# Relative-bias attention and a mixture of adapters on one core: uncast loads in 1 KB runs with Pool casting, 1024-column exp groups, and the probability-value product in a two-bank tile

## The chip, the cores and the metric

The kernel runs on one core of one Trainium2 chip. The metric is the device time of one execution in microseconds (us); smaller is better. Where several runs are given, the number is their median. The engines are called PE (TensorE, matrix products), ACT (ScalarE), Vector (DVE in the profile), Pool (GpSimd), and Sync (SP); each works through its own instructions in order. A DMA is issued by one of these engines and then carried out by the DMA engines.

A run is called slow when it is more than 1.5% above the fastest run of the same kernel. Ratios below are the mean time of one kernel's fast runs over that of the other's fast runs of the same rounds on the same chip, so they are not quite the ratios of the medians that are quoted. The interval behind a ratio is a 95% one.

## The reference

```python
# q, k, v: (B=8, H=8, S=576, D=64) float32; bias_table: (32, 8)
scores = (1 / sqrt(D)) * q @ k.T
scores = scores + bias_table[bucket(|i - j|)]          # one bucket from a distance of about 128 on
attn   = softmax(scores) @ v
x      = attn.transpose(0, 2, 1, 3).reshape(4608, 512)
logits = x @ w_gate                                    # 8 experts, the best 2 are kept
w      = softmax of the 2 kept logits
out    = x + sum over the 2 experts of w * ((x @ A[e]) @ B[e])   # A: 512x16, B: 16x512
```

The output is 4608 x 512 float32.

## The kernel before

The kernel walks over 32 pairs of heads, 4 pairs in each of 8 batches. For a pair, PE makes the scores, ACT takes the exponential out of PSUM into bf16 tiles `p`, Vector multiplies the part near the diagonal by a table of exponentials of the bias (the "band"), PE multiplies by `v` with a column of ones appended, and Vector divides by the sum that this column gives (the "normalisation"). The adapter part of the previous batch is cut into pieces, and the loop puts one piece behind a score group while pieces are left. The last 64 tokens of each head (576 = 4 x 128 + 64) are the "tail" and are handled two heads at a time.

Loads go through Pool and are cast from float32 to bf16 by the DMA:

```python
def load(dst, src, b, h0, h1, cols=None):
    for j in range(4):                     # 128 tokens on 128 partitions, 4 such blocks
        o = dst[:, j, h0:h1, :D]
        nc.gpsimd.dma_start(
            out=o, in_=src[b, h0:h1, j * 128:(j + 1) * 128, :]
            .rearrange("h p d -> p h d"))
```

The band multiply has both inputs in SBUF (the on-chip memory). The normalisation comes in two parts, because PV fills two PSUM tiles:

```python
nc.vector.tensor_tensor(pm[:, :, q0:q1], pm[:, :, q0:q1],
                        Mh[:, :, x0:x0 + q1 - q0], op=ALU.mult)          # the band
...
nc.vector.reciprocal(rc, acc[:, :, :, D])                                # norm_main: 3 blocks
nc.vector.tensor_tensor(x[:, 0:3, 2 * hp:2 * hp + 2, :], acc[:, :, :, :D],
                        rc.unsqueeze(3).to_broadcast((128, 3, 2, D)), op=ALU.mult)
...                                                                      # norm_rest: 2 blocks, with a mask
```

The output of an adapter tile goes through one of three SBUF buffers and is stored by Sync's queue, which carries nothing else after the start:

```python
op = ctx.enter_context(tc.tile_pool(name="outs", bufs=3))
...
o = op.tile([128, Dm], FP32, name="o", tag="o")
nc.vector.tensor_tensor(o, ps, xs[b][:, t].rearrange("p h d -> p (h d)"), op=ALU.add)
nc.sync.dma_start(out=out[n0:n0 + 128, :], in_=o)
```

In an odd batch a fifth tile follows, with the tails of two batches (`m_outt`, output `o<-dlt`); it takes a buffer from the same three.

The main loop, cut:

```python
for i in range(NPAIR + 1):
    b, hp = divmod(i, HP)                                # HP = 4
    if hp == 0 and b + 1 < B:                            # next batch's loads
        alloc_nat(b + 1); load_tails(b + 1); load_kq(b + 1, 0, H)
    ...
    for g in range(5):
        sc = qk(i, g); softmax_exp(i, g, sc)             # 4 groups of 1152 columns, 1 of 640
        if g == 0: transposes(i + 1)
        if g == 1: norm_main(i - 1, pv_main(i - 1))
        if g == 2: norm_rest(i - 1, pv_rest(i - 1))      # hp == 0: queue += pieces(previous batch)
        if g in (0, 3, 4) and queue: queue.pop(0)()
        band(i, g)
```

The softmax here doesn't subtract the row's maximum and nothing guards it: scores larger than these inputs give would overflow.

## Time and profile before

The time before is a median of 259.1 us (258.2 to 260.7, three runs).

| | before |
|---|---|
| profiled span | 257.7 us |
| first exp / second exp start | 28.6 / 30.2 us |
| normalisation of the first pair / of the last pair starts | 37.9 / 240.1 us |
| one pair on average, from pair 4 to pair 31 | 6.60 us |
| drain after the last normalisation | 17.6 us |

The page's first part gives, for each engine, the busy microseconds, their share of the span and the number of instructions:

```profile
PE 189.7 (74%) x2576; PEld 120.1 (47%) x2576; DVE 205.9 (80%) x641; ACT 165.4 (64%) x174; POOL 117.3 (46%) x155
```

Its second part cuts the span into 40 equal slices and gives the busy share of each in tenths (9 is 90% or more):

```profile
PE   0020698797878868897799778987898788888852
...
DVE  3200678999898888999979898989998889989972
ACT  2000469897769767886688677867796678868100
POOL 8997999745733591185508560549052000000000
```

In the first four slices only Pool is busy throughout, issuing loads and preparing tiles; from the seventh on Vector stands at 7 to 9, mostly 8 or 9, until the drain. The page also names the chain of work that ended last, as shares of the span by engine:

```profile
DVE 50%; PE 26%; ACT 7%; POOL 6%; issue 5%; DMA 3%; ACTq 0%; POOLq 0%; DVEq 0%
```

Half of the chain is Vector and almost none is DMA. Two windows of two batches each show the same. The columns are the window, its length, busy microseconds (and instructions) of PE, PEld, Vector, ACT and Pool, the granted PE clock, the DMA engines' busy share, and GB/s:

```profile
54.50:109.00 54.50, 45.60 (x660) 29.46 (x659) 49.10 (x153) 41.78 (x45) 26.49 (x33) 1.00 1.12 100
109.00:163.50 54.50, 46.15 (x638) 29.43 (x638) 48.75 (x152) 40.44 (x44) 26.08 (x32) 0.97 1.15 107
```

Vector is busy about 49 of 54.5 us, PE 46. Two lines of the waits (who waited for whom: us in total, times, longest): Vector's main wait was for PE's PV product:

```profile
DVE rcA L347 <- PE pvA L304: 9.9, 25, 1.4
...
DVE o L457 <- DMA out_dram<-o: 0.8, 1, 0.8
```

Last, from the timeline (start, duration, engine, line, operation), the first exp, a band multiply alone, and one next to a cast on Pool:

```profile
28.63 1.13 ACT L275 ACTIVATE p_227<-sc 128x1152 bf16<-128x1152 f32 x1 [23.40 <-PE sc L262]
...
31.48 0.42 DVE L289 TENSOR_TENSOR p_227<-p_227,M 128x512 bf16<-128x512 bf16 x1
...
36.40 0.60 POOL L214 CAST Bb<-B_f 128x512 bf16<-128x512 f32 x1
...
36.49 0.80 DVE L289 TENSOR_TENSOR p_282<-p_282,M 128x512 bf16<-128x512 bf16 x1
```

The same multiply took 0.42 us alone and 0.80 us when it began 0.09 us after a Pool cast had.

### The profile page before, as it was taken

What the parts mean: (1) busy time and instruction counts of PE and PEld (TensorE: products, weight loads), DVE (VectorE), ACT (ScalarE), POOL (GpSimd) and SP (SyncE); (2) the same over time, 40 slices, a digit from 0 to 9 for tenths busy, and PEclk for the clock granted to TensorE, in tenths of its full rate; (3) what the DMA queues carried; (4) which work ended last, traced back from release to release, by engine and by line L of the source; (5) the groups of instructions that cost most, each with busy time, mean ns of one, the idle gap of its engine ahead of it and who ended that gap; (6) DMA issues with size and microseconds to landing.
All of it is one profiled execution on the core that took longest, in us unless ns stands there. A gap on an engine that the chain in (4) does not pass through costs nothing.

```text
span 257.7 us, 6522 instructions
## 1 busy us (share of the span) xinstructions
PE 189.7 (74%) x2576; PEld 120.1 (47%) x2576; DVE 205.9 (80%) x641; ACT 165.4 (64%) x174; POOL 117.3 (46%) x155
## 2 busy tenths in 40 slices
PE   0020698797878868897799778987898788888852
PEld 0010255465545655456356554564465544664710
DVE  3200678999898888999979898989998889989972
ACT  2000469897769767886688677867796678868100
POOL 8997999745733591185508560549052000000000
PEclk9999999999999999999889999999999999999965
DMA  4999999969893999399939992799969003202205
GB/s 27 141 154 153 94 131 114 137 42 99 85 201 54 105 84 84 122 146 85 163 95 107 58 142 34 133 166 101 147 109 69 0 3 123 84 3 83 85 21 183
DMA packets 124759, 25.56 MB, mean 99 GB/s; under 512 B 118960, under 2 KB 119992, under 8 KB 124728
## 3 DMA queue, kind: packets, MB, share of 16 engines
q0 software_dynamic: 112768, 14.16, 89.6%
q1 hardware_dynamic: 11960, 10.97, 14.6%
q8 instruction: 20, 0.33, 0.5%
q14 instruction: 11, 0.09, 0.1%
HBM read 29.84 MB, written 9.45 MB: 152 GB/s over the span
## 4 chain that ended last, share of the span: by engine, by line
DVE 50%; PE 26%; ACT 7%; POOL 6%; issue 5%; DMA 3%; ACTq 0%; POOLq 0%; DVEq 0%
PE pvA L310 11%; DVE x L348 6%; PE sc L262 5%; DVE x L360 3%; DVE kqT L250 3%; DMA vn_86<-in_v_dram 3%; DVE o L457 3%; DVE xT L377 3%; PE pvA L304 2%; PE kqps L247 2%; DVE rcA L347 2%; POOL qn L69 2%; DVE rmB L358 2%; PE sc L258 1%; PE dl L455 1%
## 5 line engine op out<-in xcount | busy, mean ns | idle before, releaser
L262 PE MATMUL sc<-kqT 64*128 64x512 bf16 x256 | 51.8, 402 | 0.0
L69 POOL DMA_DIRECT2D kn<-in_k_dram x36 | 31.2, 896 | 19.1 <-PE kqps L247 18.2
L69 POOL DMA_DIRECT2D qn<-in_q_dram x36 | 31.0, 906 | 1.6 <-DMA vn_86<-in_v_dram 1.5
L258 PE MATMUL sc<-tlT_184,kqT 128*128 128x128 bf16 x64 | 14.5, 226 | 18.3 <-DVE kqT L250 13.0
L69 POOL DMA_DIRECT2D vn_87<-in_v_dram x16 | 14.0, 894 | 28.4 <-PE pvB L336 28.4
L69 POOL DMA_DIRECT2D vn_86<-in_v_dram x16 | 14.0, 896 | 27.7 <-PE pvB L336 27.6
L262 PEld LDWEIGHTS <-kqT 64*128 64x128 bf16 x256 | 12.4, 93 | 26.5 <-issue 17.4
L250 DVE COPY kqT<-kqps 128x1024 bf16<-128x1024 bf16 x32 | 21.8, 683 | 3.5 <-PE kqps L247 3.4
L457 DVE TENSOR_TENSOR o<-dl,x 128x512 f32<-128x512 f32 x32 | 21.8, 683 | 1.6 <-DMA out_dram<-o 0.8
L258 PEld LDWEIGHTS <-kqT 128*128 128x128 bf16 x128 | 12.8, 100 | 17.7 <-DVE kqT L250 13.2
L348 DVE TENSOR_TENSOR x<-pvA,rcA 128x384 bf16<-128x384 f32 x32 | 17.8, 557 | 1.1
L455 PE MATMUL dl<-Bb,zT 128*128 128x512 bf16 x32 | 13.3, 421 | 6.8 <-DVE zT L449 2.8
L275 ACT ACTIVATE p_227<-sc 128x1152 bf16<-128x1152 f32 x1 | 1.1, 1131 | 23.4 <-PE sc L262 23.4
L239 DVE COPY tlT_184<-tps 64x512 bf16<-64x512 bf16 x8 | 3.4, 419 | 15.4 <-POOL tlT_184 L221 15.3
L258 PE MATMUL sc<-tlT_186,kqT 128*128 128x128 bf16 x64 | 14.2, 222 | 1.7 <-ACT p_571 L275 0.7
L360 DVE TENSOR_TENSOR x<-pvB,rmB 128x256 bf16<-128x256 f32 x32 | 13.6, 424 | 1.1
L347 DVE RECIPROCAL rcA<-pvA 128x6 f32<-128x6 f32 x32 | 6.2, 195 | 10.1 <-PE pvA L304 9.9
L247 PE MATMUL kqps<-ident,kn 128*128 128x128 bf16 x128 | 13.3, 229 | 1.0 <-DVE o L457 0.6
L412 ACT ACTIVATE ex<-df 128x32 f32<-128x32 f32 (+1 forms) x12 | 2.7, 222 | 17.0 <-DVE df L409 17.0
L234 PE MATMUL tps<-ident,tl 128*128 128x128 bf16 x32 | 3.4, 232 | 13.3 <-DMA tl<-in_q_dram 13.3
L247 PE MATMUL kqps<-ident,qn 128*128 128x128 bf16 x128 | 13.1, 228 | 0.0
L247 PEld LDWEIGHTS <-kn 128*128 128x128 bf16 x128 | 8.2, 101 | 7.5 <-issue 6.8
(1431 smaller groups left out, 655.4 us busy)
## 6 DMA issues: line engine op xcount, KB each, us to landing
out_dram<-o SPq DMA_DIRECT2D x32, 256.0 KB, 2.1
kn<-in_k_dram POOLq DMA_DIRECT2D x28, 128.0 KB, 4.1
qn<-in_q_dram POOLq DMA_DIRECT2D x28, 128.0 KB, 4.7
vn_86<-in_v_dram POOLq DMA_DIRECT2D x16, 128.0 KB, 5.1
vn_87<-in_v_dram POOLq DMA_DIRECT2D x16, 128.0 KB, 4.4
out_dram<-o SPq DMA_DIRECT2D x8, 128.0 KB, 4.6
Mr<-g_d SPq DMA_DIRECT2D x1, 576.0 KB, 6.6
tl<-in_k_dram POOLq DMA_DIRECT2D x8, 64.0 KB, 4.0
```

The costliest lines, as they stand in the source:

```text
L69: nc.gpsimd.dma_start(out=o, in_=src[b, h0:h1, j * 128:(j + 1) * 128, :] .rearrange("h p d -> p h d"))
L247: nc.tensor.transpose(ps[:, w, j * 128:(j + 1) * 128], n[:, j, 2 * hp:2 * hp + 2, :], ident)
L250: nc.vector.tensor_copy(t, ps)
L258: nc.tensor.matmul(sc[:, 1024:1152], lhsT=t[:, 0, g * 128:(g + 1) * 128], rhs=tt[:, hp, 1, :], start=True, stop=True)
L262: nc.tensor.matmul(sc[:, h * 512:(h + 1) * 512], lhsT=t[s, 0, g * 128:(g + 1) * 128], rhs=t[s, 1, :], start=True, stop=True)
L310: nc.tensor.matmul(acc[:, qb, h, :], lhsT=p[:, o:o + 128], rhs=vn[:, g, 2 * hp + h, :], start=first, stop=False, skip_group_check=True)
L347: nc.vector.reciprocal(rc, acc[:, :, :, D])
L348: nc.vector.tensor_tensor(x[:, 0:3, 2 * hp:2 * hp + 2, :], acc[:, :, :, :D], rc.unsqueeze(3).to_broadcast((128, 3, 2, D)), op=ALU.mult)
L360: nc.vector.tensor_tensor(x[:, 3:5, 2 * hp:2 * hp + 2, :], acc[:, :, :, :D], rm.unsqueeze(3).to_broadcast((128, 2, 2, D)), op=ALU.mult)
L377: nc.vector.tensor_copy(xT[:, :, half * 256:(half + 1) * 256], ps)
L455: nc.tensor.matmul(ps, lhsT=zT[:, t, :], rhs=Bb, start=True, stop=True)
L457: nc.vector.tensor_tensor(o, ps, xs[b][:, t].rearrange("p h d -> p (h d)"), op=ALU.add)
```

## The change

The change has two halves.

**The load half.** Four consecutive tokens lie on one partition, so a head's q or k row block comes in runs of 1 KB. The loads are uncast float32, issued by Sync, and Pool casts one pair ahead of use. The order of tokens inside a block of 128 is therefore permuted; the bias tables are built in that order, and each output tile is stored by four DMAs. `v` is loaded uncast as well, by 16 DMAs of 32 partitions. The weights of the adapters are loaded at pair 1, behind the loads for batch 1, and cast on Pool at pair 2. Pool also builds the bias tables of pairs 1 to 3, one pair ahead, which Vector built before.

**The compute half.** Every pair has five exp groups of 1024 columns; tail against tail is done once per batch. PV has a PSUM tile of its own over two banks and one normalisation of 640 columns. Band multiplies are issued one group late. Three operations of the gate go from Vector to Pool.

The core of the diff (cut; PV's inner loops, table building and start order are left out):

```diff
-            nc.gpsimd.dma_start(
-                out=o, in_=src[b, h0:h1, j * 128:(j + 1) * 128, :]
-                .rearrange("h p d -> p h d"))
+    def load_kq(b, h0, h1):
+        for t, src in zip(kfs[b], (k, q)):
+            nc.sync.dma_start(
+                out=t[:, h0:h1, :],
+                in_=src[b, h0:h1, :S4, :].rearrange("h (p j) d -> p h (j d)", j=4))
+    def load_v(b, h0, h1):
+        vr = v[b, h0:h1, :S4, :].rearrange("h (t p j) d -> j t p h d", t=4, j=4)
+        for j in range(4):
+            for t in range(4):
+                nc.sync.dma_start(out=vfs[b][j * 32:(j + 1) * 32, t, h0:h1, :], in_=vr[j, t])
+    knp = ctx.enter_context(tc.tile_pool(name="nat", bufs=3))
+    def cast_kq(i, engs=None):
+        t = knp.tile([128, 2, 4, 2, D], BF16, name="kqn", tag="kqn")
+        for w in range(2):
+            o = t[:, w].rearrange("p j h d -> p h j d")
+            s = kfs[b][w][:, 2 * hp:2 * hp + 2, :].rearrange("p h (j d) -> p h j d", j=4)
+            nc.gpsimd.tensor_copy(o, s)                  # first pair: Vector and ACT instead
+    def cast_v(i):
+        nc.gpsimd.tensor_copy(vns[b % 2][:, :, h, :D], vfs[b][:, :, h, :])
 ...
-        n = 1152 if g < 4 else 640
+        p = pp.tile([128, 2 * S4], BF16, name=f"p{g}", tag=f"p{g}")
+        nc.scalar.activation(p, sc, ACT.Exp, scale=scale)
 ...
+    def norm(i):
+        nc.vector.reciprocal(rc, at(acc, D, (SLOT, 5), (D1, 2)))
+        nc.vector.tensor_tensor(rm, rc, mask, op=ALU.mult)
+        nc.vector.tensor_tensor(xs[b][:, :, 2 * hp:2 * hp + 2, :],
+                                at(acc, 0, (SLOT, 5), (D1, 2), (1, D)),
+                                rm.unsqueeze(3).to_broadcast((128, 5, 2, D)), op=ALU.mult)
 ...
-        nc.vector.tensor_tensor(df, lg, ...)             # and two more operations of the gate
+        nc.gpsimd.tensor_tensor(df, lg, ...)
 ...
-        nc.sync.dma_start(out=out[n0:n0 + 128, :], in_=o)
+        orr = out[n0:n0 + 128, :].rearrange("(u j) d -> j u d", j=4)
+        for j in range(4):
+            nc.sync.dma_start(out=orr[j], in_=o[j * 32:(j + 1) * 32])
 ...
+            if i == 1:
+                load_weights()
             if hp == 0 and b + 1 < B:
+                load_kq(b + 1, 0, H)
+                load_v(b + 1, 0, H)
+                load_tails(b + 1)
+            if i + 2 < NPAIR:
+                cast_kq(i + 2)
+            cast_v(i)
+            if i == 2:
+                cast_weights()
```

## The prediction

> **What bounds it now.** From the busy tenths and timeline:
> (1) Start: the first exp begins at 28.6 us. The chain of waits runs through Pool: casting loads (0.9 us per issue), then the tail tiles, cleared only at 24.4.
> (2) Steady state: in three two-batch windows from 54.5 to 218 (6.8 us per pair) Vector is busy 49.1, 48.8 and 49.9 of 54.5 us, PE 46, ACT 41. Its one sizeable listed wait is the PV reciprocal on PE (8.9 us in 164). Vector is the limit.
> (3) Drain: from 238.7, 19 us of serial MoE pieces.
>
> **On Vector, per pair** (group means; instructions overlap, so one removed is worth its mean less 70 ns):
> - normalisation 195+557+176+162+424 becomes one reciprocal, one mask, one 640-column multiply (estimate from the slope 424 to 557: 825): -0.14 us;
> - group 3's extra band multiply (215): -0.15;
> - tail copies 419+419+424 per batch become one of 683: -0.11; a new 512-column tail band: +0.09;
> - three gate operations move: -0.13.
> Together -0.44 of 6.1. Later bands and PV's own banks should remove most of the reciprocal wait: -0.2.
>
> **Taken back.** Pool gains three casts per pair; casts of this size took 662 and 603 ns. The Trainium skill (SBUF — State Buffer, "Who interferes with whom") says that a Vector instruction with two SBUF inputs contends with a Pool instruction that reads SBUF; the later one blocks. The trace agrees once: the band multiply at 36.5, during a Pool cast, took 796 ns against 420. With 1.9 us of casts and five bands per pair I estimate +0.2 to 0.5. Net about -0.45 us per pair, 28 pairs: -13 us.
>
> **ACT and PE.** Exps go from 4x1131+~705 to 5x~1025 ns plus a quarter of a 512-column exp: neutral. PE keeps its matmul count.
>
> **Start.** q and k need no Pool for loading. Packets in the trace: 2 KB 86 ns, 768 B 41; my estimate is 48 for 1 KB, 18 for 256 B uncast, so batch 0 needs about 11 us on 16 engines. But pair 1's transposes stand before the second score group on PE and need heads 2 to 7, queued behind all of v: second exp at about 18, not 30. About -10 us.
>
> **New waits.** Loads and stores now share one queue. The Trainium skill (DMA: Bandwidth & Descriptors, "Queues, rings and completion order") says each engine consumes a ring in order: no run shows it yet. At batches 4 and 6 the last stores of an odd batch stand behind 11 us of loads, and that batch's tail output needs such a store's buffer (three buffers): Vector may stall up to 6 us, twice. Charged: +6. Four stores per tile (0.6 to 0.7 us per issue) and Pool's gates lengthen the drain: +2.
>
> **Sum.** 259 - 10 - 13 + 6 + 2 = 244, shaded to **242 us, range 228 to 254**. Faster by over 2%: 0.86; within 2%: 0.10; slower: 0.04.
>
> **Signs.** Right: first exp near 9, second near 18; steady pair 6.2 to 6.5; Vector still busiest; some bands at 0.7 to 1.1 us beside Pool casts; Vector idle before an odd batch's tail output, waiting for an output DMA. Wrong: bands all at 420/550; no store waits (then about 232); Pool over 80% busy and PE waiting for casts (then 250 or more); ACT over 90%.
>
> **What would make it wrong.** Permuted casts much slower than 0.65 us; slower 256 B packets; late weights holding Pool.

## The result and the profile after

The changed kernel takes 288.0 us (287.1 to 290.1, four runs). The ratio to before is 1.112 (1.104 to 1.120): slower by 11%, where 242 us had been predicted.

| | before | after |
|---|---|---|
| profiled span | 257.7 | 286.4 |
| first exp / second exp start | 28.6 / 30.2 | 8.7 / 19.7 |
| first normalisation starts | 37.9 | 29.8 (-8.1) |
| from the first to the last normalisation | 202.2 | 236.2 (+34.0) |
| drain | 17.6 | 20.4 (+2.8) |

The three differences add up to the 28.7 us between the spans. So the start got shorter and the loop much longer. The page's first part after the change:

```profile
PE 195.4 (68%) x2603; PEld 132.1 (46%) x2608; DVE 204.6 (71%) x496; ACT 163.6 (57%) x184; POOL 113.1 (39%) x218
```

Vector's busy time is the same to 1.3 us, PE's is 5.7 us longer (and 12 us that of its weight loads, which overlap it), ACT's and Pool's are shorter. Most of the longer loop is idle time. The tenths say where:

```profile
PE   2149760997797686089698869239689778887550
...
DVE  5217823998998973178889887067979999889750
...
POOL 8263906947523914005704760400923380020100
PEclk9999996699999979669799968859979999999955
```

There are three holes. PE falls to 0 in slices 7 and 17 and to 2 and 3 in slices 26 and 27, and Vector falls to 3, 1 and 0 there. The granted clock of PE is also lower in or next to them; what that alone costs in time was not measured. The Trainium skill ("TensorE: Matmul & The Clock Gate", Part 1, on the HAM clock gate) says that the clock is halved once PE has been idle for a few microseconds. This trace agrees: PE stood idle from 112.1 to 121.6 us, and the granted clock was 1.00 from 112 to 116, 0.52 from 116 to 120 and 0.50 from 120 to 124. An undisturbed window of 30 us has a granted clock of 1.00, the two with holes have 0.88 and 0.80 (columns as in the windows before):

```profile
60.00:90.00 30.00, 24.84 (x388) 17.46 (x389) 28.63 (x66) 23.71 (x26) 12.71 (x22) 1.00 0.54 110
90.00:120.00 30.00, 17.79 (x230) 12.11 (x229) 17.06 (x43) 15.45 (x18) 13.05 (x24) 0.88 0.76 166
180.00:210.00 30.00, 16.48 (x224) 11.73 (x221) 17.76 (x41) 13.30 (x15) 11.88 (x21) 0.80 0.44 70
```

The chain that ended last has changed its composition:

```profile
DVE 35%; PE 19%; DMA 15%; SPq 15%; issue 7%; ACT 3%; POOL 3%; DVEq 0%; ACTq 0%; POOLq 0%
```

DMA and Sync's queue together are 30% of it, where DMA had 3% before. And the waits name the places:

```profile
DVE o L506 <- DMA out_dram<-o: 22.6, 3, 10.8
...
POOL df L433 <- DVE m_4302 L431: 18.1, 1, 18.1
...
DVE p_536 L342 <- POOL M L214: 9.7, 1, 9.7
...
POOL Ab L265 <- DMA A_f<-in_moe_A_dram: 8.0, 1, 8.0
```

Measured as the time between the normalisations of successive pairs, plain pairs now take 5.7 to 5.9 us, less than before. But two pairs take 17.9 us (from 104.5) and 17.4 us (from 173.0), the third 14.4 us (from 35.7), and most last pairs of a batch 8.1 to 10.5 us.

**The long pairs.** Sync's queue around the first of them (the second column is the time over which the group of DMAs was issued):

```profile
103.52 1.06 SPq L84 DMA_DIRECT2D kf<-in_k_dram  x1
104.67 0.53 SPq L84 DMA_DIRECT2D qf<-in_q_dram  x1
105.30 12.28 SPq L92 DMA_DIRECT2D vf<-in_v_dram  x16
117.68 5.57 SPq L494 DMA_DIRECT2D out_dram<-o  x12
123.34 1.20 SPq L509 DMA_DIRECT2D out_dram<-o  x2
```

and Vector's output copies at the same time; the bracket is the idle time before an instruction and what ended it:

```profile
109.38 0.68 DVE L489 TENSOR_TENSOR o<-dl,x 128x512 f32<-128x512 f32 x1
...
120.89 0.69 DVE L506 COPY o<-dlt 128x512 f32<-128x512 f32 x1 [10.82 <-DMA out_dram<-o]
```

Issuing the 18 loads for batch 4 occupies Sync from 103.5 to 117.6. The stores of three output tiles, made while that went on, wait behind them, and with three buffers full, Vector cannot write the fourth output until the first of these stores has landed. PE then has no bands and no normalisation to follow.

The wait is in Sync's order of instructions: once issued, a quarter-tile store landed after 1.7 us in the median and 3.6 at most. Busy DMA engines act on it at most through Sync's own waits, which are part of why issuing takes so long (who waited for whom: us in total, times, longest):

```profile
SPq L92 <- DMA qf<-in_q_dram: 10.5, 6, 2.6
```

By the packed trace, Sync's DMAs in this program signal completion on eight semaphores in rotation, and each waits until the DMA eight before it has landed. Here the eighth load of `v` stood until 113.3 for the landing of q.

**The third pair.** Pool waits 8.0 us for the weights before it can cast them. The bias table of the fourth pair stands behind those casts in Pool's order, and Vector waits 9.7 us for that table.

**The last pairs of a batch.** The multiplies of the band became longer, and most where Pool works off a row of casts. Vector first:

```profile
97.52 2.11 DVE L342 TENSOR_TENSOR p_1603<-p_1603,M 128x512 bf16<-128x512 bf16 x1
```

and Pool at the same time:

```profile
97.58 0.67 POOL L128 CAST kqn<-kf 128x512 bf16<-128x512 f32 x1
98.14 0.67 POOL L128 CAST kqn<-qf 128x512 bf16<-128x512 f32 x1
98.69 0.67 POOL L139 CAST vn_100<-vf 128x512 bf16<-128x512 f32 x1
99.25 0.85 POOL L128 CAST kqn<-kf 128x512 bf16<-128x512 f32 x1
```

This band took 2.11 us instead of 0.42, and it ended only after three casts had. Such rows of casts arise where Pool has waited and the casts that have piled up behind run back to back. One such wait is that of the gate's operations for Vector (once for 18.1 us), which stand in Pool's order too; others are for loads (3.6 us for a batch's q at 87.3). `gdve` below tests how much the gate's part is. Of the 168 band multiplies, the 75 that ran beside some Pool instruction carry all of the excess. The excess of all 168 over the lengths that they have undisturbed (548, 418 and 284 ns for 768, 512 and 256 columns; the group means of before are 554, 420 and 291) is 18.3 us, or 0.57 us per pair.

### The profile page after: what moved, and what is told of

Same layout as the page of the kernel before. It is cut to its first block, busy times and chain, and to the rows that moved or that the text cites. A ratio compares the mean times of both kernels' runs of the same rounds, so it can differ in the third digit from the quotient of the medians.

```text
span 286.4 us, 6863 instructions
## 1 busy us (share of the span) xinstructions
PE 195.4 (68%) x2603; PEld 132.1 (46%) x2608; DVE 204.6 (71%) x496; ACT 163.6 (57%) x184; POOL 113.1 (39%) x218
## 4 chain that ended last, share of the span: by engine, by line
DVE 35%; PE 19%; DMA 15%; SPq 15%; issue 7%; ACT 3%; POOL 3%; DVEq 0%; ACTq 0%; POOLq 0%
DMA vf<-in_v_dram 9%; PE pv L358 8%; DVE x L383 7%; SPq L92 7%; DVE kqT L281 3%; DMA out_dram<-o 3%; SPq L494 3%; DVE o L489 3%; DMA g_d<-ge 2%; DVE rm L382 2%; PE sc L315 2%; PE xps L399 2%; SPq L84 2%; PE sc L319 2%; DVE rc L380 2%
## 5 line engine op out<-in xcount | busy, mean ns | idle before, releaser
L279 PE MATMUL kqps<-ident,kqn 128*128 128x128 bf16 x256 | 23.2, 237 | 24.3 <-POOL kqn L128 19.4
L279 PEld LDWEIGHTS <-kqn 128*128 128x128 bf16 x256 | 16.1, 105 | 33.5 <-POOL kqn L128 22.4
L399 PE MATMUL xps<-ident,x 128*128 128x128 bf16 x128 | 12.7, 242 | 23.9 <-DVE o L506 18.7
L383 DVE TENSOR_TENSOR x<-pv,rm 128x640 bf16<-128x640 f32 x32 | 26.4, 825 | 1.1
L128 POOL CAST kqn<-kf 128x512 bf16<-128x512 f32 x31 | 24.1, 776 | 5.8 <-DMA kf<-in_k_dram 5.7
L128 POOL CAST kqn<-qf 128x512 bf16<-128x512 f32 x31 | 22.1, 711 | 9.2 <-DMA qf<-in_q_dram 9.2
L487 PE MATMUL dl<-Bb,zT 128*128 128x512 bf16 x31 | 13.1, 431 | 10.4 <-DVE zT L481 6.6
L506 DVE COPY o<-dlt 128x512 f32<-128x512 f32 x4 | 2.8, 691 | 23.4 <-DMA out_dram<-o 22.6
L315 PEld LDWEIGHTS <-kqT 64*128 64x128 bf16 x256 | 12.5, 94 | 15.0 <-issue 3.2
L319 PE MATMUL sc<-kqT,tlT 128*128 128x512 bf16 x32 | 13.1, 411 | 5.2 <-ACT p_4328 L327 0.8
L116 POOL DMA_DIRECT2D vt_99<-in_v_dram x8 | 4.9, 621 | 22.7 <-PE pv L358 22.7
L323 PE MATMUL sc<-tlT,kqT 128*128 128x128 bf16 x128 | 13.4, 232 | 0.0
L116 POOL DMA_DIRECT2D vt_96<-in_v_dram x8 | 4.9, 618 | 19.9 <-PE pv L358 19.9
L401 DVE COPY xT<-xps 128x1024 bf16<-128x1024 bf16 x16 | 10.9, 683 | 2.1 <-PE xps L399 2.1
```

What stands on the lines that cost most here:

```text
L128: nc.gpsimd.tensor_copy(o, s)
L279: nc.tensor.transpose(o[:, :, j, :], n[:, w, j], ident)
L315: nc.tensor.matmul(sc[:, h * 512:(h + 1) * 512], lhsT=t[s, 0, g * 128:(g + 1) * 128], rhs=t[s, 1, :], start=True, stop=True)
L319: nc.tensor.matmul(sc[:, 0:512], lhsT=tt[:, 0, hp, :], rhs=t[:, 1, :], start=True, stop=True)
L323: nc.tensor.matmul(sc[:, o:o + 128], lhsT=t[:, 0, j * 128:(j + 1) * 128], rhs=tt[:, 1, hp, :], start=True, stop=True, skip_group_check=True)
L383: nc.vector.tensor_tensor(xs[b][:, :, 2 * hp:2 * hp + 2, :], at(acc, 0, (SLOT, 5), (D1, 2), (1, D)), rm.unsqueeze(3).to_broadcast((128, 5, ...
```

## The experiments

Twelve kernels were run, with three or more timed rounds in each. All but `noread`, which is wrong, are correct. The table gives medians of all runs. The kernels ran on four chips; the median of the kernel before was 258.9 to 259.5 us on each of them.

| label | what it is | us | range | ratio to before |
|---|---|---|---|---|
| o8 | after, 8 output buffers | 261.3 | 259.1 to 262.3 | 1.007 (1.000 to 1.013) |
| wearly | after, weights loaded before batch 1 | 288.2 | 287.7 to 288.8 | 1.111 (1.105 to 1.117) |
| o8w | both | 260.8 | 260.4 to 261.0 | 1.006 (1.001 to 1.010) |
| noread | o8w, Pool's casts become memsets | 233.2 | 232.3 to 233.4 | 0.899 (0.894 to 0.903) |
| o8c5 | o8, weights cast at pair 5 | 256.1 | 252.8 to 258.3 | none, see below |
| n2 | o8c5, two buffers for the cast q and k | 247.0 | 246.3 to 247.3 | 0.952 (0.949 to 0.956) |
| gdve | o8c5, gate back on Vector | 252.9 | 251.8 to 253.0 | 0.974 (0.971 to 0.978) |
| hyb | the compute half alone | 239.6 | 239.2 to 239.8 | 0.924 (0.921 to 0.927) |
| hybcast | hyb plus Pool copies of q, k, v | 274.0 | 271.9 to 277.1 | 1.053 (1.044 to 1.062) |
| n2s | n2, another order of the first loads | 245.4 | 244.2 to 247.1 | 0.946 (0.939 to 0.954) |
| mix | hyb, first batches loaded uncast | 240.6 | 239.6 to 241.0 | 0.927 (0.922 to 0.931) |
| actq | after, 24 stores from ACT's queue | 276.5 | 274.8 to 279.2 | 1.065 (1.059 to 1.070) |

### Do the stores wait in the queue? (o8)

The theory was that stores behind loads fill the three output buffers. With eight, all outputs of a batch fit while the loads hold the queue. The rival was that late weights, or Pool's casts, made the loop longer.

```diff
-    op = ctx.enter_context(tc.tile_pool(name="outs", bufs=3))
+    op = ctx.enter_context(tc.tile_pool(name="outs", bufs=8))
```

> The changed kernel with eight output buffers instead of three; nothing else. Theory A (stores queued behind loads hold Vector through the output buffers): Vector's two waits of 10.8 us for an output store vanish and so do the two pairs of 17.9 and 17.4 us (plain pairs 5.8): time about 265 us (288 less 23, range 262 to 269). Theory B (Pool and Vector block each other at the shared SBUF port and the store wait only fills time that is lost anyway): the wait moves elsewhere and the time stays above 280.

It took 261.3 us, 26.7 us less than after and just below the expected range. The two long pairs shrank from 17.9 and 17.4 us to 6.3 and 7.0, which is 22.0 of the 26.7; the third pair shrank from 14.4 to 12.5. So the waits for the buffers were the largest loss. But the kernel is still no faster than before, and 19 us above the prediction, although a cost that the prediction had charged was gone.

### Does loading the weights earlier help? (wearly, o8w)

```diff
-            if i == 1:
+            if i == 0:
                 load_weights()
```

> The changed kernel with the MoE weights' loads issued before the second batch's loads instead of after them; nothing else. Theory A: Pool's wait for A_f (8.0 us) and Vector's 9.7 us wait for the fourth bias table vanish: about 280 us (288 less 8, range 277 to 283). Rival: the second batch's loads come about 5 us later and Pool then waits for them just as long: 286 to 289.

> Both edits. If the two waits are independent the savings add: about 257 us (range 253 to 261). If both fill the same slack: no more than 3 us below the better single edit.

`wearly` took 288.2 us, the same as after. `o8w`, which has the eight buffers too, took 260.8, the same as `o8`. The line of Pool's wait for the weights is gone, but the third pair still took 13.8 us in `wearly` and 11.7 in `o8w`. In `wearly` a cast stood waiting in the same place, now for batch 1's q, which the weights had pushed back:

```profile
40.98 0.62 POOL L128 CAST kqn<-qf 128x512 bf16<-128x512 f32 x1 [4.14 <-DMA qf<-in_q_dram]
```

A load was moved ahead of another in the same queue, and the wait moved to the other. That did not refute the theory that the third pair is held by Pool's waiting; it showed that the edit could not test it. `o8c5` did.

### What do Pool's reads of SBUF cost? (noread against o8w)

The Trainium skill ("SBUF — State Buffer", section "Who interferes with whom") says that a Vector instruction with two SBUF inputs contends with a Pool instruction that reads SBUF, and not with one that only writes it, and that the second one blocks fully. This experiment keeps Pool's three instructions per pair, and their writes, but takes their reads away. Its result is wrong (relative error 0.94).

```diff
-                nc.gpsimd.tensor_copy(o, s)
+                nc.gpsimd.memset(t[:, w], 0.0)
 ...
-        nc.gpsimd.tensor_copy(vns[b % 2][:, :, h, :D], vfs[b][:, :, h, :])
+        nc.gpsimd.memset(vns[b % 2][:, :, h, :D], 0.0)
```

> Both edits, and Pool's three casts per pair replaced by memsets of the same output tiles: Pool writes as before but reads no SBUF. The result is wrong on purpose. Port theory: all bands fall to 418 and 548 ns (band excess of 18 us goes to about 1) and the time falls 12 to 20 us below the run with both edits. Rival (what slows the bands is Pool's writes or its mere activity): bands keep their long tail and the time stays within 5 us.

It took 233.2 us against 260.8. The two larger band groups of `o8w` (busy us, mean ns, then the idle time before them and what ended it):

```profile
L342 DVE TENSOR_TENSOR p<-p,M 128x512 bf16<-128x512 bf16 x64 | 38.6, 603 | 2.4 <-POOL M L214 2.4
L342 DVE TENSOR_TENSOR p<-p,M 128x768 bf16<-128x768 bf16 x64 | 37.6, 603 | 0.0
```

and of `noread`, with its memsets:

```profile
L342 DVE TENSOR_TENSOR p<-p,M 128x768 bf16<-128x768 bf16 x64 | 35.0, 562 | 0.0
L128 POOL MEMSET kqn<- 128x512 bf16 x62 | 31.6, 557 | 0.1
...
L342 DVE TENSOR_TENSOR p<-p,M 128x512 bf16<-128x512 bf16 x64 | 28.1, 439 | 0.7 <-POOL M L214 0.7
```

Pool still runs three instructions per pair (557 ns for a memset of q or k, where the casts took 669 and 766), but the bands are back at almost their undisturbed lengths (the 256-column ones too, from 447 to 282 ns): the excess falls from about 20.9 to 2.2 us. In the trace of `noread`, 22 bands ran beside nothing but a memset on Pool, and none of them was more than 0.01 us longer than undisturbed. The trace agrees with the page: it is reading, not being busy, that holds Vector up. The whole difference of 27.6 us is not contention, though. A memset waits for no load, so waits for loads vanish too; 9.8 us of the difference lie before the fifth pair, where those waits are. The other 17.8 us are close to the 18.7 us of excess.

### Does Pool's in-order wait hold the third pair? (o8c5)

Here the cast of the weights goes from pair 2 to pair 5, when they have long landed and the bias tables are all built. No load moves.

```diff
-            if i == 2:
+            if i == 5:
                 cast_weights()
```

> Eight output buffers, loads in the order of the changed kernel, and the weights' cast on Pool moved from the third pair to the sixth. Theory: with three output buffers out of the way, the 12.5 us that the third pair takes is Pool waiting for the weights; moving the cast lets Pool go on to the bias table and the next casts, and no load comes later (as it did when the weights were loaded early, which gained nothing): about 254 us (261 less 7, range 251 to 257). Rival: the third pair waits for the second batch's q and k in any case: within 2 us of 261.

The third pair fell from 12.5 to 6.1 us. Vector's wait for Pool's bias tables, 9.4 us in `o8` with 7.7 at the longest, became (us in total, times, longest):

```profile
DVE p L342 <- POOL M L214: 1.7, 2, 0.9
```

The four runs spread from 252.8 to 258.3 us, and two of them (257.4 and 258.3) count as slow, so there is no interval. Against `o8` the kernel gained 5.1 us by the medians of all runs, and 7.5 us with the two fast runs alone (253.8). The theory holds: what cost time was the wait that stood before the bias table in Pool's order.

### Are the rows of casts the cost of contention? (n2, gdve)

Two ways of breaking the rows up were tried, both on `o8c5`. `n2` gives the cast q and k two buffers instead of three, so that Pool cannot cast a pair before PE has transposed the pair two before it. `gdve` puts the gate's three operations back on Vector, so that Pool does not wait there.

```diff
-    knp = ctx.enter_context(tc.tile_pool(name="nat", bufs=3))       # n2
+    knp = ctx.enter_context(tc.tile_pool(name="nat", bufs=2))
```

```diff
-        nc.gpsimd.tensor_tensor(df, lg, ...)                        # gdve: and the two other gate operations
+        nc.vector.tensor_tensor(df, lg, ...)
```

> As the run before, with two instead of three buffers for the cast q and k, so that Pool cannot run two pairs ahead and cast six times in a row. If the 2.1 us bands come from runs of casts back to back, they go (longest band about 1.1 us) and the time falls 3 to 7 us. If only the number of casts matters, the bands' total stays and the time changes by less than 2 us. If Pool is too late, PE's wait for casts grows and the time rises.

> As the first run of this call, with the three small gate operations back on Vector. Prediction's theory: each costs Vector about 0.12 us more per use, 12 uses of three: time rises about 4 us. Rival: they hold Pool (it waits up to 17 us at the first of them and then works off its casts in a burst) and cost Vector hand-overs: time falls by 2 to 6 us.

`n2` took 247.0 us: 9.1 us less than `o8c5` by all runs, 6.8 us by its fast runs. Two lines of `o8c5`, a band group and Pool's cast of k:

```profile
L342 DVE TENSOR_TENSOR p<-p,M 128x512 bf16<-128x512 bf16 x64 | 41.5, 648 | 1.7 <-POOL M L214 1.7
...
L128 POOL CAST kqn<-kf 128x512 bf16<-128x512 f32 x31 | 23.9, 772 | 5.7 <-DMA kf<-in_k_dram 5.7
```

and the same two of `n2`:

```profile
L342 DVE TENSOR_TENSOR p<-p,M 128x512 bf16<-128x512 bf16 x64 | 31.9, 498 | 1.2 <-POOL M L214 1.2
...
L128 POOL CAST kqn<-kf 128x512 bf16<-128x512 f32 x31 | 24.0, 774 | 27.3 <-PE kqps L279 19.8 <-DMA kf<-in_k_dram 7.5
```

The number and length of the casts are the same, but in `n2` each now waits for PE's transposes (19.8 us of waits that `o8c5` lacks), and so they are spread. The excess of the bands fell from 22.6 to 13.9 us, the longest band from 2.16 to 1.17 us, and the last pairs of a batch from up to 10.5 to at most 8.1 us. One buffer less is faster here, because it paces an engine that does harm when it runs ahead.

`gdve` took 252.9 us. I had expected moving the operations back to cost 4 us; instead it is 3.2 us below `o8c5` by all runs and 0.9 us by its fast runs. It did not cost anything that these runs can show; whether it gained is not settled, since `o8c5` itself spread by 5.6 us. Its trace does show what the gate does to the rows: `o8c5` has six bands of over 2 us, `gdve` one, and the excess is 17.4 us instead of 22.6. The gate thus makes most of the longest bands, but most of the excess is there without it.

### Is the compute half worth what was predicted? (hyb)

`hyb` takes the changed kernel and puts the loads of before back: cast by the DMA, issued by Pool, tokens in natural order, one store per tile, three output buffers. The bias tables are built on Vector again. The compute half stays, with the gate on Pool.

```diff
-            nc.sync.dma_start(
-                out=t[:, h0:h1, :],
-                in_=src[b, h0:h1, :S4, :].rearrange("h (p j) d -> p h (j d)", j=4))
+        for j in range(4):
+            nc.gpsimd.dma_start(
+                out=dst[:, j, h0:h1, :D], in_=src[b, h0:h1, j * 128:(j + 1) * 128, :]
+                .rearrange("h p d -> p h d"))
 ...
-            if i + 2 < NPAIR:
-                cast_kq(i + 2)
-            cast_v(i)
 ...
-        orr = out[n0:n0 + 128, :].rearrange("(u j) d -> j u d", j=4)
-        for j in range(4):
-            nc.sync.dma_start(out=orr[j], in_=o[j * 32:(j + 1) * 32])
+        nc.sync.dma_start(out=out[n0:n0 + 128, :], in_=o)
```

> The compute part of the change alone on the loads of before: q, k and v cast by Pool's DMAs in natural token order, no casts on Pool, one store per tile, three output buffers, bias tables on Vector; five 1024-column exp groups, two-bank PV, late bands and gates on Pool as changed. If the loads (1 KB runs, casts on Pool) are what costs, and the compute part is worth the 0.6 us per pair of Vector that was predicted, this is about 240 us (range 235 to 246). If the casting loads' packets, which kept the 16 engines busy for about 26 us per batch before, become the limit: 248 to 255. If the compute part is worth nothing: 257 to 261.

It took 239.6 us, a ratio of 0.924, and beats both kernels. The first normalisation starts at 37.9 us, as before; from pair 4 to pair 31 a pair takes 6.07 us, 0.53 less than before. The page's first part of `hyb`, and its two larger band groups:

```profile
PE 183.5 (77%) x2608; PEld 122.7 (52%) x2608; DVE 185.9 (78%) x502; ACT 161.1 (68%) x182; POOL 135.8 (57%) x213
```

```profile
L311 DVE TENSOR_TENSOR p<-p,M 128x768 bf16<-128x768 bf16 x64 | 34.5, 556 | 0.0
...
L311 DVE TENSOR_TENSOR p<-p,M 128x512 bf16<-128x512 bf16 x64 | 26.9, 421 | 0.3 <-ACT p L296 0.3
```

Vector's busy time fell from 205.9 to 185.9 us, 0.62 us per pair, and the bands have their undisturbed lengths although Pool is busier (135.8 us) than in the changed kernel (113.1): issuing casting loads did not hold Vector up, casting in SBUF did.

### Pool's reads put on top of hyb (hybcast)

`hybcast` adds copies on Pool of q, k and v (already bf16) for each pair, on the path from load to use.

```diff
+            nc.gpsimd.tensor_copy(t[:, w], nat[b][w][:, :, 2 * hp:2 * hp + 2, :])
 ...
+        nc.gpsimd.tensor_copy(vns[b % 2][:, :, h, :D], vraw[b][:, :, h, :])
```

> The compute part on the loads of before (239.6 us), with the changed kernel's three Pool passes per pair put back as a detour and nothing else: Pool copies the already cast q, k and v of each pair from the loaded tiles to the tiles that PE reads. No load, queue or layout changes. If Pool's reads block the bands, as the run without reads said, band means go from 556, 421 and 280 ns to above 600, 600 and 370 and the time rises by 12 to 22 us (252 to 262). If the changed kernel's slowness came only from load order and queues, the time stays within 3 us of 240.

It took 274.0 us (272.4 by its three fast runs). The bands became long again:

```profile
L326 DVE TENSOR_TENSOR p<-p,M 128x768 bf16<-128x768 bf16 x64 | 45.8, 732 | 0.8 <-ACT p L311 0.6
L326 DVE TENSOR_TENSOR p<-p,M 128x512 bf16<-128x512 bf16 x64 | 31.6, 494 | 0.4 <-ACT p L311 0.4
```

The excess rose from about 0.7 to 19.6 us, in a profile that fell on the slow one of the four runs. The rise in time is larger, 33 us, and beyond the 12 to 22 expected. Two other things differ, which no run separates: Pool, which here also issues all loads, is busy for 196.6 us, and the first normalisation comes only at 46.7 us, 8.8 us later than in `hyb`. So it confirms the direction, and its size must not be read as the price of contention alone.

### Can the fast start be had as well? (n2s, mix)

`n2s` takes `n2` and puts all q and k of batch 0 ahead of v, with the bias table's store between two halves of v. `mix` takes `hyb` and loads q and k of batches 0 and 1, and v of batch 0, uncast in natural order through Sync; q and k of the first two pairs are cast on Vector and ACT, the rest on Pool.

```diff
-    load_v(0, 0, H)                       # n2s
     load_kq(0, 2, H)
+    load_v(0, 0, H, (0, 1))
 ...                                       # after the bias table's store
+    load_v(0, 0, H, (2, 3))
```

```diff
-    load_kq(0, 0, 2)                      # mix: DMA-cast loads of batch 0 and 1 replaced
+    load_raw_kq(0, 0, 2)
 ...
+    load_raw(vraw, v, 0, 0, H)
+    load_raw_kq(1, 0, 4)
```

> The repaired change (eight output buffers, late weight cast, two cast buffers: 247.0 us) with the start's queue reordered: all of q and k of batch 0 before v, and the bias table's store between two halves of v. The second exp should come at about 13 us instead of 19.7 and the time fall 4 to 7 us (240 to 243). If the start is bound elsewhere (batch 1's loads), it falls by less than 2 us.

> The compute part on casting loads, but with q and k of batches 0 and 1 and v of batch 0 loaded uncast in natural order and cast by the engines that are idle at the start. First normalisation at about 22 us instead of 37.9, then the DMA engines limit: 229 to 234 us (239.6 less 6 to 10). If the casting loads of the later batches cannot keep up, the gain is given back: 237 to 240.

`n2s` took 245.4 us; its range overlaps that of `n2`, so the gain of 1.6 us is not sure. Its second exp came at 14.8 us instead of 19.7, but at the fifth pair's normalisation it was already behind `n2` (53.7 against 52.3 us). `mix` took 240.6 us against 239.6 for `hyb`, measured on another chip: no gain. Its first normalisation starts at 33.6 us instead of 37.9, but by the fifth pair it is at 58.1, where `hyb` is at 57.2. So the earlier start was lost within the first batch. `mix` brings some casts on Pool back (excess of the bands 4.8 us), so it does not show what holds the first batch of `hyb`.

### Is it the queue, or the DMA engines behind it? (actq)

With eight buffers the stores still wait; they only hurt nobody. To see whether the order in Sync's queue was the cause, 24 of the 136 stores (tiles 2 to 4 of batches 1 and 3, ahead of the two long pairs) were issued by ACT. The three buffers stay.

```diff
-            nc.sync.dma_start(out=orr[j], in_=o[j * 32:(j + 1) * 32])
+            eng = nc.scalar if b in (1, 3) and t > 0 else nc.sync
+            eng.dma_start(out=orr[j], in_=o[j * 32:(j + 1) * 32])
```

> The changed kernel with its three output buffers; only the stores of the second to fourth tile of batches 1 and 3 (24 of 136) are issued from ACT's queue instead of Sync's, so that they do not stand behind the loads of batches 4 and 6. If the order in one queue makes the two waits of 10.8 us: they shrink below 2 us and the time is 262 to 268, as with eight buffers. If the 16 DMA engines being full with loads makes them, the stores stay slow from the other queue too: waits of 6 us or more remain and the time is above 275.

It took 276.5 us (276.3 by its three fast runs), 11.8 us less than after in fast runs. Two of its waits, and one of Sync's own:

```profile
DVE o L507 <- DMA out_dram<-o: 8.3, 3, 3.7
...
ACT p L327 <- DMA out_dram<-o: 7.9, 4, 3.0
```

```profile
SPq L92 <- DMA out_dram<-o: 17.8, 4, 7.8
```

Vector's wait for a buffer fell from 22.6 to 8.3 us in total, and the long pairs from 17.9 and 17.4 to 10.5 and 10.4. The place of the stores in Sync's order is thus the larger part. The rest is not settled. Stores landed up to 5.2 us after their issue (3.6 in the changed kernel), so loads in flight may have slowed them. ACT stalled for up to 3.0 us before an exp, and just then it was issuing four stores, which took 3.9 us. And the two queues did not come apart: in this program ACT's and Sync's DMAs share the eight semaphores in rotation, and Sync stood up to 7.8 us before a load of `v` until a store had landed. The result lies between what the two theories would give alone, and the edit was not a clean test of them.

## Why the prediction was wrong

The prediction was 242 us, and the time was 288.0. The term that failed most is the +6 for stores behind loads (step 5): taking that wait away was worth 26.7 us. Next come contention with its rows of casts (step 4) and Pool's wait for the weights, charged with nothing (step 6). The steps, one by one:

1. **What bounds the kernel before: right.** Taking 20.0 us of work off Vector (`hyb`, which also has 6.2 us less of PE's) took 19.4 us off the time.
2. **The start: right in mechanism, nearly right in size.** First and second exp at 8.7 and 19.7 us (predicted: near 9 and near 18). The first normalisation came 8.1 us earlier (predicted: 10). The estimates of packet times hold: 1 KB took 46 ns in the median (estimate 48), uncast 256 B 18 ns in the median (estimate 18) and 23 in the mean.
3. **Work removed from Vector: right.** Predicted 0.44 of work and 0.2 of waiting, 0.64 us per pair; measured with `hyb`, 0.62 of busy time and 0.53 of time. The 640-column multiply took 0.82 us, as estimated.
4. **"I estimate +0.2 to 0.5" for contention: the mechanism right, the size too small.** It was 0.57 us per pair in the changed kernel, and so it ate the whole 0.53. The estimate treated casts as single events spread over the pair. It missed that Pool, waiting in order for the gate or for loads, lets casts pile up, and that a band which meets a row of them waits for three, not for one (2.11 us). Removing the rows (`n2`) gave 7 to 9 us.
5. **"Vector may stall up to 6 us, twice. Charged: +6": the waiting instruction right, its cause in part and its size wrong, and the largest error of the sum.** Removing the wait (`o8`) took off 26.7 us. The prediction had rested on each DMA engine working off its ring in order, and on 11 us of transfers. No run here shows the rings to be what held the stores: they waited to be issued, while Sync took 14.2 us to issue a batch's 18 loads, and landed soon after (1.7 us in the median); single waits reached 10.8 us; each long pair lost about 11 us, since everything behind Vector's output stood still; and PE's granted clock was lower in the windows with these stalls. The prediction also took for its total only half of its own upper bound.
6. **"late weights holding Pool": named as what would make it wrong, and charged with nothing.** Casting them at pair 5 took off 5 to 7.5 us. The program could have shown the danger: the change puts three bias tables, the weights' casts and three casts per pair on one in-order engine within three pairs, some behind a load that is itself behind 18 others.
7. **The drain: about right.** +2.8 us (predicted +2).

As an account of the 46 us that were missing: 20.7 are step 5 beyond the 6 charged, 14.3 are steps 4 (its rows) and 6 together (`o8` to `n2`), and 11 are left. Of those, 2 are the start, 2 the shading from 244 to 242, and 1 the drain. The remaining 6 are not assigned by any run; the contention left in `n2`, 13.9 us in all, is some 4 us more than what the middle of the prediction's range amounts to over 28 pairs. Removals need not add up exactly, so this is an account and not a proof.

The load half as a whole, which was predicted to gain about 10 us at the start for 8 us of queueing and drain and its share of contention, cost 48.4 us (`hyb` against after). Even repaired (`n2s`) it stays 5.8 us behind `hyb`. In the traces of these two the first normalisation starts 9.3 us earlier, the loop takes 10.9 us more, and the drain 4.0 us more. The first is what uncast loads through Sync give, in the order of `n2s`. The contention that is left is more than the second (excess of 16.5 us in `n2s`, 0.7 in `hyb`), but that it is the cause was not tested. The third may come with four stores per tile, but no run isolates it.

## What to carry to other kernels

Before work moves to an idle engine, look at what it waits for there, in order, and whether it reads SBUF beside a Vector instruction with two SBUF inputs; here a pass that "costs nothing" on Pool ate 0.57 us per pair. Before stores share an issuing engine with bulk loads, count the output buffers that are filled while one burst of loads is being issued, and give that many (26.7 us here), or issue the stores elsewhere (11.8 us here, for the 24 that were moved). And when a change has two halves, run each alone: the compute half was worth 19.4 us, and the bundle hid it.

## What the Trainium skill lacked or had wrong

- "SBUF — State Buffer", section "Who interferes with whom": right about reading (excess of 2.2 us with writing Pool instructions, about 20.9 with reading ones). It lacks what happens with a row of Pool instructions: a band that by the profile began 0.06 us before the first of four casts ended only after the third, and took 2.11 us instead of 0.42. Four more bands in that trace took about as long. Why it was not let in earlier is not shown.
- "DMA: Bandwidth & Descriptors", section "Queues, rings and completion order": it speaks of the order in which a DMA engine takes descriptors from a ring, which no run here tests. What held the stores comes before the rings, and the section lacks it: the issuing engine's own order. Sync took 14.2 us to issue 18 uncast loads of 3 MB together, and stores behind them kept their output buffers for that time.
- The same page, section "Issuing engines are not separate DMA queues": it says that issuing from several engines saves only the issue time, which is usually small beside the DMA itself. Here that time, with the issuing engine's own waits in it, was not small: with 24 of the 136 stores issued by ACT, so that they no longer stood behind the 14.2 us in which Sync issues a batch's loads, the kernel took 11.8 us less of 288.
- The same page has no figure that we found for the price of casting in a DMA for small packets: a packet of 256 B took 32 ns when cast to 128 B, and 18 ns in the median uncast.
